# Row spreading on TensorE, shared PSUM banks, more weight gates, dummy matmuls and paired k r blocks in an RWKV5 plus squared-ReLU kernel

## The chip, the cores and the metric

The kernel runs on one core of one Trainium2 chip. The metric is the device time of one execution in microseconds (us). Each kernel is executed several times; I give the median and the range. A run counts as slow when it is more than 1.5% above the fastest run of the same kernel, and fast runs are compared with fast runs. The profile is one execution; its span is 1.8 us shorter than the device time of the same execution (before: 180.6 against 182.37 us).

Names of engines: PE is TensorE (matmul), PEld its weight loads, DVE VectorE, ACT ScalarE, POOL GpSimd, SP SyncE, which issues most loads. "Hardware queue" below is the queue of the loads that SP issues, "software queue" that of the weight slices, which POOL issues.

## The reference, cut to what matters

```python
# r, k, v: (4, 8, 768, 48) fp32;  w, u: (8, 48);  w_in: (384, 2048);  w_out: (2048, 384)
for t in range(S):
    kt, vt, rt = k[:, :, t], v[:, :, t], r[:, :, t]
    cur = einsum('bhd,bhe->bhde', u * kt, vt)
    y[:, :, t] = einsum('bhd,bhde->bhe', rt, state + cur)
    state = w * state + einsum('bhd,bhe->bhde', kt, vt)
x = y.transpose(0, 2, 1, 3).reshape(3072, 384)
h = maximum(x @ w_in, 0)
out = (h * h) @ w_out
```

The kernel cuts the sequence into 24 units: 6 chunks of 128 positions for each of 4 batches. Unit i is chunk i // 4 of batch i % 4. A unit needs k, r and v of its chunk. Its bonus term is `v * du`, where `du` is the sum over d of r k u. Two units make a pair, whose 256 rows go through the two feed-forward layers together.

## The kernel before

Nothing is scheduled by hand. The kernel describes each piece of work as a step with an engine, an estimated duration, the steps it needs, a priority, and the buffers that it takes (`alloc`) and gives back (`free`). A planner then plays a rough simulation and writes out the instructions in the order in which they started there.

```python
def order_steps(steps, pools, sw_rate=0.75, hw_rate=0.17):
    ...
        for e in ENGINES:
            ...
            for s in ready[e]:
                need = {}
                for _, p in s.alloc:
                    need[p] = need.get(p, 0) + 1
                if any(len(slots[p]) < n for p, n in need.items()):
                    continue                      # its buffers are not free yet
                if s.dma and out[e] >= 8:
                    continue
                if best is None or s.prio < best.prio:
                    best = s
    ...
    order.sort(key=lambda s: s.start)

PLAN = dict(per=6.2, loads=['k0', 'r0', 'v0', 'ub', 'k1', 'r1', 'v1', 'wcol',
            'kP1', 'rP1', 'vP1', 'kP2', 'rP2', 'vP2', ...],   # k0: of unit 0;  kP1: of units 2 and 3
            gates=[('v', 2), ('v', 2)], ..., lead=-1, f1lag=0.5, f2lag=8, ...)
POOLS = dict(ldr=2, ldk=2, ldv=2, rk=6, P0=4, ..., rkT=6, bank=3, bankH=3, bankO=2, Bm=3, ...)
```

A buffer of `ldv` holds v of a whole pair, one half for each unit. There are two of them, so pair 2 (units 4 and 5) takes the buffer of pair 0 (units 0 and 1). A load of a pair allocates its buffer:

```python
            Ld[x, 2 * p] = Ld[x, 2 * p + 1] = st(
                "ld" + item, "SP", 0.5, dma=2.05, alloc=[(var, "ld" + x)], emit=go, ...)
        else:
            def go(x=x, i=i, var=var):
                nc.sync.dma_start(out=ld[x][slot[var]][:, i % 2], in_=single[x][i % B, i // B])
            Ld[x, i] = st("ld" + item, "SP", 0.4, dma=1.04, prio=-150 + n, emit=go,
                          alloc=[(var, "ld" + x)] if i % 2 == 0 else [])
    ...
    for part in range(2):                        # the weights: two gates, four slices behind each
        ...
            nc.gpsimd.tensor_copy(gate[:, part : part + 1], ld[x][...][0:1, i % 2, 0, 0:1])
    ...
        dv[i] = st(f"dv{i}", "DVE", 0.56, [du[i], Ld["v", i], vb[i]], ...,     # v * du
                   free=[f"vP{g}"] if i % 2 else [], emit=f_dv(i))
        A = st(f"A{i}", "PE", 0.42, [rkT[i]], ...,                             # k r, 8 matmuls of 48 rows
               alloc=[(f"bA{i}0", "bank"), (f"bA{i}1", "bank")], emit=f_A(i))
```

A gate is a copy of one element of a load, written into POOL's order ahead of the weight slices, so that the slices are asked for only after that load has landed. In this kernel the only single loads are those of units 0 and 1.

Of the kernel before, what the change touches and what calls it, by code (L numbers as in the profile page):

```python
# [10 lines left out]
FP32 = mybir.dt.float32  # L11
# [4 lines left out]

class Step:
    def __init__(s, name, eng, dur, deps=(), prio=0.0, lat=0.08, alloc=(), free=(), dma=0.0, shared=False, emit=None):
        s.name = name
        s.eng = eng  # L20
        s.dur = dur
        s.deps = [d for d in deps if d is not None]
        s.prio = prio
        s.lat = lat
        s.alloc = list(alloc)
        s.free = list(free)
        s.dma = dma
        s.shared = shared
        s.emit = emit


ENGINES = ("PE", "ACT", "DVE", "POOL", "SP")


def order_steps(steps, pools, sw_rate=0.75, hw_rate=0.17):
# [14 lines left out]
    count = [0]  # L50

    def push(t, k, o):
        count[0] += 1
        heapq.heappush(ev, (t, count[0], k, o))
# [5 lines left out]
    slots = {k: list(range(n)) for k, n in pools.items()}  # L60
# [5 lines left out]
    clock = [0.0]  # L66
    order = []

    def rates():
        return (hw_rate, sw_rate) if rings["SP"] and rings["POOL"] else (1.0, 1.0)  # L70

    def advance(t):
        while clock[0] < t - 1e-9:
            if not rings["SP"] and not rings["POOL"]:
                clock[0] = t
                return
            rh, rs = rates()
            dt = t - clock[0]
            for q, r in (("SP", rh), ("POOL", rs)):
                if rings[q]:  # L80
                    dt = min(dt, rings[q][0][1] / r)
            clock[0] += dt
            for q, r in (("SP", rh), ("POOL", rs)):
                if rings[q]:
                    rings[q][0][1] -= dt * r
                    if rings[q][0][1] < 1e-7:
                        push(clock[0] + 1.2, "d", rings[q].pop(0)[0])

    def landing():
        rh, rs = rates()  # L90
        c = [rings[q][0][1] / r for q, r in (("SP", rh), ("POOL", rs)) if rings[q]]
        return clock[0] + min(c) if c else None
# [12 lines left out]
    while True:  # L105
# [5 lines left out]
        while ev and ev[0][0] <= t + 1e-9:  # L111
            _, _, k, o = heapq.heappop(ev)
            if k == "r":
                ready[o.eng].append(o)
            elif k == "f":
                slots[o[0]].append(o[1])
            elif k == "e":
                idle[o.eng] = True
                if not o.dma:
                    finish(o, t)  # L120
            elif k == "q":
                rings[o.eng].append([o, o.dma])
            elif k == "d":
                out[o.eng] -= 1
                finish(o, t)
        for e in ENGINES:
# [3 lines left out]
            for s in ready[e]:  # L130
                need = {}
                for _, p in s.alloc:
                    need[p] = need.get(p, 0) + 1
                if any(len(slots[p]) < n for p, n in need.items()):
                    continue
                if s.dma and out[e] >= 8:
                    continue
                if best is None or s.prio < best.prio:
                    best = s
# [15 lines left out]
            for v, p in s.alloc:  # L155
                where[v] = given[v] = (p, slots[p].pop(0))
            ready[e].remove(s)
            order.append(s)
            if s.dma:
                out[e] += 1  # L160
                push(s.end + 1.0, "q", s)
# [3 lines left out]
    return order, {v: i for v, (_, i) in given.items()}  # L165


PLAN = dict(per=6.2, loads=['k0', 'r0', 'v0', 'ub', 'k1', 'r1', 'v1', 'wcol', 'kP1', 'rP1', 'vP1', 'kP2', 'rP2', 'vP2', 'kP3', 'rP3', 'vP3', 'kP4', 'rP4', 'vP4', 'kP5', 'rP5', 'vP5', 'kP6', 'rP6', 'vP6', 'kP7', 'rP7', 'vP7', 'kP8', 'rP8', 'vP8', 'kP9', 'rP9', 'vP9', 'kP10', 'rP10', 'vP10', 'kP11', 'rP11', 'vP11'], nprep=8, p1set=2, nT=8, nX=8, gates=[('v', 2), ('v', 2)], sq=(1, 3, 5, 7), ldlead=26, lead=-1, f1lag=0.5, f2lag=8, relup=-3, sqp=-2)
POOLS = dict(ldr=2, ldk=2, ldv=2, rk=6, P0=4, dv=3, vb=8, rkT=6, bank=3, bankH=3, bankO=2, Bm=3, xs=3, xT=2, hr=6, hq=28, os=3, ts=2)
# [3 lines left out]
def kernel(  # L173
# [31 lines left out]
    def flat_rows(src):  # L205
        return bass.AP(tensor=src.tensor, offset=src.offset, ap=[[0, 128], [1, H * D]])
# [30 lines left out]
    first = {"bank": 0, "bankH": POOLS["bank"], "bankO": POOLS["bank"] + POOLS["bankH"]}  # L237

    def bank(var, pool):
        return banks[first[pool] + slot[var]]  # L240

    def heads(var, pool, n):
        return bank(var, pool).rearrange("p (a b) -> p a b", a=HP)[:, :, 0:n]
# [7 lines left out]
    wb = const.tile([128, H, D], FP32, name="wb")  # L251
    ub = const.tile([128, H, D], FP32, name="ub")
    wcol = const.tile([128, HP], FP32, name="wcol")
    logw = const.tile([128, H, D], FP32, name="logw")
    Wkhat = const.tile([128, H, D], FP32, name="Wkhat")
    Wt2 = const.tile([128, H, D], FP32, name="Wt2")
    WLm = const.tile([128, HP, 2 * D], FP32, name="WLm")
    gate = const.tile([1, 16], FP32, name="gate")

    tcol_i = const.tile([128, 1], mybir.dt.int32, name="tcol_i")  # L260
# [25 lines left out]
    nc.vector.memset(wcol, 1.0)  # L286
# [4 lines left out]
    steps = []  # L291
    PE_LAT = 0.25
    per = PLAN["per"]

    def st(name, eng, dur, deps=(), **kw):
        s = Step(name, eng, dur, deps, **kw)
        steps.append(s)
        return s

    def load_wcol():  # L300
        for e in range(2):
            nc.sync.dma_start(
                out=wcol[64 * e : 64 * e + D, :], in_=w.rearrange("(a e) d -> e d a", e=2)[e]
            )

    def make_WLm():
        nc.scalar.activation(wcol, wcol, AF.Ln)
        nc.scalar.activation(wcol, wcol, AF.Exp, scale=float(L))

    def fill_WLm():  # L310
        for e in range(2):
            col = wcol[64 * e : 64 * e + D, :]
            nc.gpsimd.tensor_copy(
                WLm[64 * e : 64 * e + D, :, D * e : D * (e + 1)],
                bass.AP(tensor=col.tensor, offset=col.offset, ap=[list(col.ap[0]), list(col.ap[1]), [0, D]]),
            )

    s_wb = st("wb", "SP", 0.1, dma=0.6, prio=-200, emit=lambda: nc.sync.dma_start(out=wb.rearrange("p a b -> p (a b)"), in_=flat_rows(w)))
    s_lw = st("logw", "ACT", 0.52, [s_wb], prio=-200, emit=lambda: nc.scalar.activation(logw, wb, AF.Ln))
    s_wk = st("Wk", "ACT", 0.61, [s_lw], prio=-199, emit=lambda: nc.scalar.activation(Wkhat, logw, AF.Exp, scale=njcol))  # L320
    s_wt = st("Wt", "ACT", 0.61, [s_wk], prio=-198, emit=lambda: nc.scalar.activation(Wt2, logw, AF.Exp, scale=tcol))

    Ld = {}
    where = {}
    n = 0
    for item in PLAN["loads"]:
        n += 1
        if item == "ub":
            Ld["ub"] = st("ub", "SP", 0.3, dma=0.6, prio=-150 + n, emit=lambda: nc.sync.dma_start(out=ub.rearrange("p a b -> p (a b)"), in_=flat_rows(u)))
        elif item == "wcol":  # L330
            Ld["wcol"] = st("wcol", "SP", 0.6, dma=0.3, prio=-150 + n, emit=load_wcol)
        elif item[1] == "P":
            x, p = item[0], int(item[2:])
            var = f"{x}P{p}"

            def go(x=x, p=p, var=var):
                nc.sync.dma_start(
                    out=ld[x][slot[var]].rearrange("p a h d -> p (a h) d"),
                    in_=both({"r": r, "k": k, "v": v}[x], p),
                )  # L340

            Ld[x, 2 * p] = Ld[x, 2 * p + 1] = st(
                "ld" + item, "SP", 0.5, dma=2.05, alloc=[(var, "ld" + x)], emit=go,
                prio=(2 * p - 2) * per - PLAN["ldlead"] + {"k": 0, "r": 0.1, "v": 0.2}[x],
            )
        else:
            x, i = item[0], int(item[1:])
            var = f"{x}P{i // 2}"

            def go(x=x, i=i, var=var):  # L350
                nc.sync.dma_start(out=ld[x][slot[var]][:, i % 2], in_=single[x][i % B, i // B])  # L351

            Ld[x, i] = st("ld" + item, "SP", 0.4, dma=1.04, prio=-150 + n, emit=go,
                          alloc=[(var, "ld" + x)] if i % 2 == 0 else [])

    s_wl = st("WLcol", "ACT", 0.45, [Ld["wcol"], s_wt], prio=-100, emit=make_WLm)
    s_wm = st("WLm", "POOL", 0.6, [s_wl], prio=-50, emit=fill_WLm)

    Ws = []
    for part in range(2):  # L360
        x, i = PLAN["gates"][part]

        def go(part=part, x=x, i=i):
            nc.gpsimd.tensor_copy(gate[:, part : part + 1], ld[x][slot[f"{x}P{i // 2}"]][0:1, i % 2, 0, 0:1])

# [351 lines left out]
```

## Time and profile before

| | before |
|---|---|
| median of 3 runs | 183.56 us (183.44 to 183.97) |
| span of the profiled run | 180.6 us |
| PE busy | 160.6 us, 89% of the span |
| granted clock, mean | 1.00 (no record before 28.22 us) |
| first matmul of the first layer | 27.48 us |
| weights' gate passed | 17.7 us |

These are lines of the profile's page: the busy time of each engine, the span in 40 equal slices (each digit is a busy share in tenths, PEclk the granted clock in tenths), and the chain of work that ended last.

```profile
span 180.6 us, 4082 instructions
PE 160.6 (89%) x1592; PEld 118.2 (65%) x1592; DVE 128.6 (71%) x216; ACT 117.5 (65%) x214; POOL 106.8 (59%) x116
...
PE   0344769899999999999999999999999999999991
...
DVE  3399998997388838959979696778777889631310
...
PEclk9999999999999999999999999999999999999999
...
PE 79%; DVE 9%; DMA 4%; ACT 2%; SPq 2%; issue 1%; DVEq 0%
```

From 40 us on (the tenth slice) PE is full, so work taken from PE there is time saved. Ahead of that VectorE is the full engine. The row PEclk says nothing of the start: the clock records in the trace of the kernel before begin only at 28.22 us, with full speed, and the views count the time ahead of the first record as full speed. The timeline shows otherwise: eight k r matmuls take 0.61 us at 23.21 us and 0.40 at 106.59. The table by stretches gives this more exactly; its columns are the stretch, its length, busy time of PE, PEld, DVE, ACT and POOL with the count of instructions, the granted clock, the DMA share (packet times summed over the time of 16 engines, so it can pass 1) and GB/s.

```profile
10.00:20.00 10.00, 5.33 (x53) 3.49 (x54) 9.87 (x17) 3.58 (x7) 6.54 (x10) 1.00 1.13 206
20.00:30.00 10.00, 7.92 (x86) 6.07 (x86) 9.08 (x17) 4.76 (x9) 9.84 (x11) 1.00 1.18 190
30.00:40.00 10.00, 8.93 (x97) 7.22 (x96) 9.49 (x19) 9.82 (x19) 2.13 (x3) 1.00 1.27 185
40.00:50.00 10.00, 10.00 (x94) 7.79 (x92) 5.98 (x10) 6.91 (x13) 6.77 (x7) 1.00 1.15 215
```

Three places of PE's timeline matter (start, duration, line, operation, tiles, shapes, count): the first first-layer matmuls, and a k r block between two others in the full stretch. The ends of matmuls are modelled, so block costs are read from start to start.

```profile
27.48 1.83 PE L604 MATMUL bank<-xT,W 128*128 128x256 bf16 x12
...
105.84 0.82 PE L604 MATMUL bank<-xT,W 128*128 128x256 bf16 x6
106.59 0.40 PE L454 MATMUL bank<-rkT 48*128 48x128 bf16 x8
106.92 0.82 PE L638 MATMUL bank<-W,hq 128*128 128x384 bf16 x4
```

The six matmuls at 105.84 are followed 0.75 us later by the k r block, whereas such a block followed by one of its own kind takes 0.655; the next block starts 0.33 later. A k r block of one unit costs 0.10 + 0.33 = 0.43 us.

### The profile page before, as it was taken

To read this page: it belongs to the slowest core of one execution; us is meant where nothing else is said; L and a number is where in the kernel's file an instruction comes from. 1 tells how busy PE (TensorE), PEld (TensorE's weight loads), DVE (VectorE), ACT (ScalarE), POOL (GpSimd) and SP (SyncE) were. 2 spreads that over 40 slices of the span, in tenths; PEclk is the share of its full clock that TensorE was granted. 3 is DMA by queue.
4 is the path that set the end of the run, shared out by engine and by line. 5 is a ranking of instruction groups with operands and counts; after the bars stand their busy time and mean duration, and the time that the engine had idled before them with its cause. 6 is when DMAs were issued, how large, how long until landed. Compare 5 with 4: busy or idle time off the path is not lost.

```text
span 180.6 us, 4082 instructions
## 1 busy us (share of the span) xinstructions
PE 160.6 (89%) x1592; PEld 118.2 (65%) x1592; DVE 128.6 (71%) x216; ACT 117.5 (65%) x214; POOL 106.8 (59%) x116
## 2 busy tenths in 40 slices
PE   0344769899999999999999999999999999999991
PEld 0222557778766867758678677677686776777760
DVE  3399998997388838959979696778777889631310
ACT  2641528986793886827776758579298495496851
POOL 2346998024940999599879977986968980000000
PEclk9999999999999999999999999999999999999999
DMA  3999999999949649979799799897896255221102
GB/s 85 207 195 216 196 191 193 184 185 222 225 116 241 149 82 253 184 152 241 142 216 204 122 237 202 138 225 164 167 228 155 71 120 80 65 65 47 41 2 87
DMA packets 105794, 28.44 MB, mean 157 GB/s; under 512 B 98864, under 2 KB 105776, under 8 KB 105776
## 3 DMA queue, kind: packets, MB, share of 16 engines
q1 hardware_dynamic: 102064, 25.04, 68.1%
q0 software_dynamic: 3712, 3.15, 11.0%
q8 instruction: 12, 0.20, 0.5%
q14 instruction: 6, 0.05, 0.1%
HBM read 20.84 MB, written 4.72 MB: 142 GB/s over the span
## 4 chain that ended last, share of the span: by engine, by line
PE 79%; DVE 9%; DMA 4%; ACT 2%; SPq 2%; issue 1%; DVEq 0%
PE bank L638 34%; PE bank L604 32%; PE bank L454 4%; PE bank L483 3%; DMA ub<-in_u_dram 2%; DMA xT<-xs 2%; PE bank L478 2%; PE bank L429 2%; DVE rk L382 2%; SPq L351 2%; DVE xs L506 2%; DVE dv L411 2%; PE bank L495 2%; DVE Bm L467 1%; ACT rkT L436 1%
## 5 line engine op out<-in xcount | busy, mean ns | idle before, releaser
L618 ACT ACTIVATE hr<-bank 128x512 bf16<-128x512 f32 x96 | 55.9, 595 | 29.4 <-PE bank L604 27.6
L604 PE MATMUL bank<-xT,W 128*128 128x256 bf16 x576 | 73.8, 273 | 0.4 <-DVE hq L629 0.3
L638 PE MATMUL bank<-W,hq 128*128 128x384 bf16 x384 | 72.0, 326 | 0.0
L604 PEld LDWEIGHTS <-W 128*128 128x128 bf16 x576 | 55.0, 98 | 11.8 <-issue 0.9
L638 PEld LDWEIGHTS <-hq 128*128 128x128 bf16 x384 | 36.1, 98 | 19.3
L629 DVE TENSOR_TENSOR hq<-bank,hr 128x512 bf16<-128x512 f32 x48 | 32.6, 683 | 17.4 <-ACT hr L618 17.4
L467 DVE TENSOR_TENSOR Bm<-bank,maskJT 128x512 bf16<-128x512 f32 x48 | 31.1, 681 | 8.2 <-PE bank L454 8.1
L388 POOL TENSOR_TENSOR P<-ldr,ldk 128x384 f32<-128x384 f32 x24 | 28.2, 1177 | 9.9 <-DMA ldr<-in_r_dram 9.9
L528 POOL TENSOR_TENSOR S0W<-ts,WLm 128x384 bf16<-128x384 f32 x16 | 16.5, 1031 | 29.1 <-DVE ts L522 28.9
L626 ACT ACTIVATE hq<-hr 128x512 bf16<-128x512 bf16 x48 | 30.2, 630 | 1.1
L397 POOL TENSOR_TENSOR P<-P,ub 128x384 f32<-128x384 f32 x22 | 22.9, 1043 | 1.4
L411 DVE TENSOR_TENSOR dv<-ldv,du 128x384 f32<-128x384 f32 x24 | 21.2, 883 | 0.5
L506 DVE TENSOR_TENSOR xs<-bank,dv 128x384 bf16<-128x384 f32 x24 | 13.3, 555 | 11.1 <-PE bank L483 10.7
L651 ACT COPY os<-bank 128x384 f32<-128x384 f32 x24 | 11.4, 476 | 12.4 <-PE bank L638 12.1
L429 PE MATMUL bank<-identity,rk 128*128 128x128 bf16 x64 | 7.5, 273 | 10.5 <-DVE rk L382 10.2
L382 POOL TENSOR_TENSOR rk<-ldr,Wt 128x384 bf16<-128x384 f32 x16 | 16.6, 1040 | 0.1
L382 POOL TENSOR_TENSOR rk<-ldk,Wkhat 128x384 bf16<-128x384 f32 x16 | 16.0, 1002 | 0.0
L429 PEld LDWEIGHTS <-rk 128*128 128x128 bf16 x64 | 5.5, 120 | 12.4 <-DVE rk L382 11.5
L417 ACT CAST vb<-ldv 128x384 bf16<-128x384 f32 x24 | 11.6, 507 | 2.9 <-DMA ldv<-in_v_dram 2.9
L403 DVE TENSOR_REDUCE du<-P 128x8 f32<-128x384 f32 x24 | 13.0, 543 | 0.2 <-POOL P L397 0.2
L454 PE MATMUL bank<-rkT 48*128 48x128 bf16 x192 | 10.6, 233 | 2.5 <-ACT rkT L436 2.2
L483 PE MATMUL bank<-vb,Bm 128*128 128x48 bf16 x192 | 12.2, 189 | 0.4 <-DVE Bm L467 0.4
(40 smaller groups left out, 101.7 us busy)
## 6 DMA issues: line engine op xcount, KB each, us to landing
out_dram<-os SPq DMA_DIRECT2D x24, 192.0 KB, 2.6
ldk<-in_k_dram SPq DMA_DIRECT2D x11, 384.0 KB, 4.1
ldr<-in_r_dram SPq DMA_DIRECT2D x11, 384.0 KB, 5.0
ldv<-in_v_dram SPq DMA_DIRECT2D x11, 384.0 KB, 4.0
W<-in_moe_w_in_dram POOLq DMA_DIRECT2D x4, 384.0 KB, 8.9
W<-in_moe_w_out_dram POOLq DMA_DIRECT2D x4, 384.0 KB, 15.6
ldk<-in_k_dram SPq DMA_DIRECT2D x2, 192.0 KB, 4.2
ldr<-in_r_dram SPq DMA_DIRECT2D x2, 192.0 KB, 4.5
```

Source lines behind the costliest of these rows:

```text
L382: e.tensor_mul(rk[slot[f"rk{i}"]][:, j, :, 0:D], ld[x][slot[f"{x}P{i // 2}"]][:, i % 2], tab)
L388: nc.gpsimd.tensor_mul(P0b[slot[f"P0{i}"]], ld["r"][slot[f"rP{i // 2}"]][:, i % 2], ld["k"][slot[f"kP{i // 2}"]][:, i % 2])
L397: (nc.vector if eng == "DVE" else nc.gpsimd).tensor_mul(t, t, ub)
L411: nc.vector.tensor_mul(dvb[slot[f"dv{i}"]], ld["v"][slot[f"vP{i // 2}"]][:, i % 2], du_b)
L454: nc.tensor.matmul(heads(f"bA{i}{e}", "bank", 128)[:, hc, :], rkT[p0 : p0 + D, HP + hc, :], rkT[p0 : p0 + D, hc, :], start=True, stop=True ...
L467: nc.vector.tensor_mul(Bmb[slot[f"Bm{i}"]][:, e], heads(f"bA{i}{e}", "bank", 128), mask_b)
L483: nc.tensor.matmul(Y[:, hc, D * e : D * (e + 1)], Bm[:, e, hc, :], vb[:, 2 * hc + e, :], start=(c == 0), stop=True, skip_group_check=True,)
L604: nc.tensor.matmul(hp[:, fi, :], W1[s // 2][:, c, 128 * f : 128 * (f + 1)], xt[:, c, :], start=(c == 0), stop=(c == CCH - 1), skip_group_c ...
L618: nc.scalar.activation(hrb[slot[f"hr{g},{s}"]], hp, AF.Relu)
L626: nc.scalar.activation(hq, hr, AF.Square)
L629: nc.vector.tensor_mul(hq, hp, hr)
L638: nc.tensor.matmul(o, hqb[slot[f"hq{g},{f // 2}"]][:, f % 2, L * j : L * (j + 1)], W2[q][:, f % 4, :], start=(f == 0), stop=(f == FCH - 1) ...
```

## The change

The intent is to begin the feed-forward part earlier and to make the k r blocks cheaper.

- w and u arrive as rows and are spread over the partitions by matmuls with a row of ones, instead of 128-row copies by DMA.
- All PSUM banks come from one list of eight, with shares (bank 4, bankH 4, bankO 3), instead of three fixed sets.
- Units 2 to 5 are loaded singly as well, in the order of need, and the eight weight slices have six gates instead of two: v of unit 2 for the first three slices, then one gate for each.
- Before the first layers begin, PE's gaps in the plan are filled with dummy matmuls on zeros.
- From unit 8 on, the k r products of two units are one block of 16 matmuls, in four banks.
- Lags and pools are tuned anew: `lead` -1 to -2, `f1lag` 0.5 to 0, `f2lag` 8 to 10; rk 6 to 4, rkT 6 to 4, Bm 3 to 2, P0 4 to 6, dv 3 to 6, xT 2 to 3.
- Two units fewer are transposed by PE (`nT` 8 to 6), and ScalarE makes 52 of the squares instead of 48.

The rest of the diff, about a thousand lines, turns closures into named functions. Its core:

```diff
@@ the planner's choice of a step @@
-                need = {}
-                for _, p in s.alloc:
-                    need[p] = need.get(p, 0) + 1
-                if any(len(slots[p]) < n for p, n in need.items()):
-                    continue
+                fits = True
+                if s.alloc:
+                    p = s.alloc[0][1]
+                    n = len(s.alloc)
+                    if p.startswith("bank"):
+                        fits = share[p] >= n and len(slots["banks"]) >= n
+                    else:
+                        fits = all(slots[p] for _, p in s.alloc)
...
-PLAN = dict(per=6.2, loads=['k0', 'r0', 'v0', 'ub', 'k1', 'r1', 'v1', 'wcol', 'kP1', 'rP1', 'vP1', 'kP2', 'rP2', 'vP2', ...
-            gates=[('v', 2), ('v', 2)], lead=-1, f1lag=0.5, f2lag=8, nT=8, ...)
+PLAN = dict(per=6.2, loads=['k0', 'r0', 'v0', 'k1', 'r1', 'v1', 'k2', 'r2', 'v2', 'k3', 'r3', 'v3', 'k4', 'r4', 'v4', 'k5', 'r5', 'v5', 'kP3', ...
+            gates=[('v', 2), ('v', 2), ('v', 2), ('k', 3), ('v', 3), ('k', 4), ('r', 4), ('v', 4)],
+            lead=-2, f1lag=0, f2lag=10, nT=6, nA=8, fill=24, ...)
...
+        if i < plan["nA"]:
+            A[i] = st(f"A{i}", "A", ((i,),), "PE", 0.43, ...)
+        elif i % 2 == 0:
+            A[i] = A[i + 1] = st(f"A{i}", "A", ((i, i + 1),), "PE", 0.66, [rkT[i], rkT[i + 1]], ...,
+                                 alloc=[(f"bA{j}{e}", "bank") for j in (i, i + 1) for e in (0, 1)])
...
+        if s.eng == "PE":
+            if s.start < min(opened, PLAN["fill"]):
+                cost = 0.45 if s.start < 5 else 0.24
+                for _ in range(int((s.start - before - 0.2) / cost)):
+                    nc.tensor.matmul(banks[7], warm[:, 0:128], warm, ...)
+            before = s.end
```

## The prediction

> **What bounds the kernel now.** From about 40 us on, TensorE (PE). The table by stretches has PE busy 10.0 of every 10 us from 40 to 160, save 9.65 in 80-90 and 9.9 in 150-160; the chain of waits gives PE 79% of the span. In the timeline a first-layer block (6 matmuls, 128x256) repeats every 0.655 us, a second-layer block (4, 128x384) every 0.65, a Y block 0.37, U 0.17; a k r block (8 matmuls on 48 rows) costs 0.43: it runs 0.33 after a 0.10 gap, though its weight loads take only 0.23. Times their counts (96, 96, 24, 20, 24, and 16 transpose blocks) that is about 153 us, my estimate of dense work. The other 27 us are start and tail. Before the first-layer matmuls begin at 27.4 us, PE does only 7 us of dense-rate work; VectorE is full there (9.9 of 10 us in 10-20, 9.1 in 20-30, 9.5 in 30-40). It waits 3.1 us for the decay table, then 1.65 for the 128-row copy of u. The weights' gate is passed at 17.7; their slices land 6.7 to 18.5 us after issue, the last near 42. The tail is 3.5 us after the last matmul.
>
> **What the change does.**
> 1. PE spreads w and u from rows: 0.39 MB leave the queue, about 2 us at 0.2 MB/us. The decay table comes no earlier, but unit 1's k and r do, and u stalls nothing.
> 2. Loads unit by unit, eight gates: the first slice is asked for at about 11.5, not 18.2; x of units 0 and 1 is done at about 18, not 21. In PE's order the first first-layer block stands behind unit 1 and the fourth rk transpose, not behind unit 3's U.
> 3. 26 dummy matmuls in gaps, all before that block. The Trainium skill's "TensorE: Matmul & The Clock Gate" (Part 1) says an idle array runs at half clock until about 3.4 us of sustained work. The trace agrees in effect: 8 k r matmuls take 0.61 us at 8.7 us, 0.40 later, though the granted clock reads 1.0. Worth below 1 us, as VectorE limits there.
> 4. Units 8 to 23: k r of two units in one block. The skill's "TensorEngine Tiling (Array Packing)", Key Properties, says a change of tiling mode drains the engine; the gap and the excess over 0.23 agree. A pair should cost 0.66, not 0.86: 1.6 us, wholly critical.
> 5. Two units fewer transposed on PE: 0.9 us. More early squares on ScalarE: 2.8 us of VectorE time.
>
> **Sum.** PE's dense work becomes 150.5 us, 4.4 of it before the first first-layer block, at about 19 us. Dense from there, PE would end at 165. Weights (2.5 to 2.8 us a slice beside loads, last near 35) and VectorE must hold it up in 19-36: I put 4.5 us, and 1 us for the four banks that a pair needs at once. PE ends at 170.5, span 174, plus 2.9 as before (183.56 against 180.6): **177 us**, range 172 to 181.5; faster by over 2%: 0.77, same 0.19, slower 0.04.
>
> **What would show it.** First first-layer matmul at 17-21 us; PE's end at 168-174, stretches from 40 us still full; blocks of 16 at about 0.66 us; weights landed near 35; the wait on u gone.
>
> **What would make it wrong.** Weights late because loads share the queue, so that PE is held on slices or on an x transpose queued ahead of ready blocks; pairs waiting for four banks; smaller pools (rk, rkT, masks) stalling PE after 40 us.

## More of the kernel before

The order in which instructions are written matters twice. Each engine executes its own instructions in that order. And an instruction that reads a buffer waits for the last write that stands ahead of it in that order.

## The result, and the profile after

The changed kernel takes 194.94 us (median of 4 fast runs, 194.13 to 195.66), and the kernel before, on the same chip, 183.74 us (183.44 to 183.97). The ratio is 1.061 with a 95% interval of 1.056 to 1.066: slower by 6%. A ratio in this document is the mean time of one kernel's fast runs over that of the other's of the same rounds, so it is not quite the ratio of the medians.

The same lines of the page, for the kernel after:

```profile
span 192.2 us, 4192 instructions
PE 166.8 (87%) x1620; PEld 121.1 (63%) x1622; DVE 120.7 (63%) x212; ACT 117.1 (61%) x218; POOL 104.8 (54%) x117
...
PE   7996000499999999999999999999999799999991
...
DVE  3943000879789669598897858969697774912210
...
PEclk9999755569999999999999999999999999999999
...
PE 79%; DMA 9%; DVE 4%; SPq 3%; POOL 2%; issue 1%; ACT 0%; DVEq 0%; POOLq 0%
```

VectorE stands still from 16.4 to 34.5 us and PE from 17.7 to 36.0, and the granted clock falls. After 40 us PE is nearly as full as before, except for one slice near 151 us. DMA has 9% of the chain of waits where it had 4%. Two lines of the table of waits (who waited for whom: total, times, longest) name the place; L543 is `v * du`, L571 the k r block, L581 the masking of its result.

```profile
PE bank L571 <- DVE Bm L581: 18.3, 1, 18.3
DVE dv L543 <- DMA ldv<-in_v_dram: 18.1, 1, 18.1
```

Each is one single wait. In VectorE's timeline (in brackets the idle time ahead of an instruction and what ended it):

```profile
15.89 0.54 DVE L538 TENSOR_REDUCE du<-P 128x8 f32<-128x384 f32 x1
34.50 0.82 DVE L543 TENSOR_TENSOR dv<-ldv,du 128x384 f32<-128x384 f32 x1 [18.07 <-DMA ldv<-in_v_dram]
```

VectorE takes its instructions in order, so the masks and x of every later unit wait behind it. The chain in order of time (start, duration, what) says which load it is; SPq L510 is the issuing of a load.

```profile
14.22 5.23 SPq L510
...
19.55 14.87 DMA ldv<-in_v_dram
...
34.50 0.82 DVE dv L543
```

And PE's timeline around the hole: the last dummies, the first k r block behind the hole, and the first first-layer block.

```profile
16.48 1.24 PE L698 MATMUL bank<-warm 128*128 128x512 bf16 x5
35.98 0.61 PE L571 MATMUL bank<-rkT 48*128 48x128 bf16 x8 [18.26 <-DVE Bm L581]
...
39.62 1.70 PE L647 MATMUL bank<-xT,W 128*128 128x256 bf16 x7
```

The first first-layer matmul starts at 39.6 us, 12.1 us later than before, and the run is 11.2 us longer. After it the two kernels go at nearly the same pace. The following table makes this visible. For each kernel I count the matmuls that PE has still to finish at a given time, multiply by what their blocks cost from start to start in a full stretch (first-layer block of six 0.655 us, second-layer block of four 0.65, Y 0.37 and 0.21 in the first chunk, U 0.17, k r 0.43 and 0.65 for a pair, the transposes of a unit 0.45 for r and k and 0.17 for x), and add the time itself. It is my estimate of where PE would end if it were dense from there. A number that rises is time lost in between.

| projected end of PE, us, seen at | 20 | 30 | 40 | 100 | 170 |
|---|---|---|---|---|---|
| before | 169.1 | 174.2 | 176.0 | 176.8 | 177.1 |
| after | 166.9 | 176.9 | 185.4 | 186.7 | 188.4 |

Seen at 20 us the kernel after is 2.2 us ahead, seen at 40 it is 9.4 behind, and at the end 11.3: nearly all of its loss falls between 20 and 40 us.

Which load does `v * du` of unit 1 (the instruction at 34.50) wait for? Unit 1's v was long there: ScalarE had cast it at 10.47 us. The load that landed at 34.4 was issued at 19.55, behind k and r of unit 5, and it is v of unit 5. The order in which the compiled kernel has them explains it. In the plan, unit 5's load of v stands at position 53, unit 1's product at 65, and unit 4's load of v, which allocates the pair's buffer, at 89. The load of unit 5 has no `alloc`, so the planner lets it go when SP is idle; its half of the pair's buffer is the half in which unit 1's v still lies. Since the load stands ahead of the product, the product waits for it. The trace has this edge itself: the product at 34.50 waits for semaphore 103, on which the loads of v of units 2 and 5 count, while unit 1's v counts on 110.

This is a wrong result, too. The product of unit 1 multiplies with unit 5's v. I worked out from the reference what that does: a relative L2 error of 0.071 on the unit's 128 rows and of 0.0147 on the whole output, which the comparison with the reference lets pass. No run showed this directly; it follows from the order of the instructions, and from the product's wait.

Theory: this one wrong edge, from the load of unit 5's v to the product of unit 1, holds VectorE, then PE, and lets PE's clock fall. It costs much only because that load lands late, among the weight slices. Rivals: (a) loads in general are late because the weights are now asked for at 11 us, so the hole would open elsewhere without the edge; (b) the dummies or the pairs hold the engines; (c) the smaller pools do.

### The profile page after: what moved, and what is told of

It is laid out like the page before. It is cut to its first block, busy times and chain, and to the rows that moved or that the text cites. A ratio compares the mean times of both kernels' runs of the same rounds, so it can differ in the third digit from the quotient of the medians.

```text
span 192.2 us, 4192 instructions
## 1 busy us (share of the span) xinstructions
PE 166.8 (87%) x1620; PEld 121.1 (63%) x1622; DVE 120.7 (63%) x212; ACT 117.1 (61%) x218; POOL 104.8 (54%) x117
## 4 chain that ended last, share of the span: by engine, by line
PE 79%; DMA 9%; DVE 4%; SPq 3%; POOL 2%; issue 1%; ACT 0%; DVEq 0%; POOLq 0%
PE bank L647 31%; PE bank L669 30%; DMA ldv<-in_v_dram 8%; PE bank L571 4%; PE bank L698 3%; SPq L510 3%; PE bank L593 2%; PE bank L589 2%; PE bank L555 2%; DMA rkT<-rk 2%; PE bank L602 2%; PE bank L462 1%; DVE dv L543 1%; DVE hq L664 1%; PE bank L628 1%
## 5 line engine op out<-in xcount | busy, mean ns | idle before, releaser
L669 PE MATMUL bank<-W,hq 128*128 128x384 bf16 x384 | 70.3, 326 | 0.1
L657 ACT ACTIVATE hr<-bank 128x512 bf16<-128x512 f32 x96 | 55.7, 596 | 19.6 <-PE bank L647 18.4
L664 DVE TENSOR_TENSOR hq<-bank,hr 128x512 bf16<-128x512 f32 x44 | 29.5, 683 | 18.7 <-ACT hr L657 18.4
L581 DVE TENSOR_TENSOR Bm<-bank,maskJT 128x512 bf16<-128x512 f32 x48 | 30.4, 683 | 13.5 <-PE bank L571 13.5
L623 POOL TENSOR_TENSOR S0W<-ts,WLm 128x384 bf16<-128x384 f32 x16 | 16.4, 1030 | 30.7 <-DVE ts L620 30.6
L662 ACT ACTIVATE hq<-hr 128x512 bf16<-128x512 bf16 x52 | 32.4, 630 | 1.0
L543 DVE TENSOR_TENSOR dv<-ldv,du 128x384 f32<-128x384 f32 x24 | 18.6, 778 | 18.7 <-DMA ldv<-in_v_dram 18.1
L535 POOL TENSOR_TENSOR P<-P,ub 128x384 f32<-128x384 f32 x23 | 25.0, 1088 | 9.0 <-DVE P L531 7.5
L571 PE MATMUL bank<-rkT 48*128 48x128 bf16 x192 | 9.1, 228 | 19.6 <-DVE Bm L581 18.3
L531 POOL TENSOR_TENSOR P<-ldr,ldk 128x384 f32<-128x384 f32 x22 | 23.2, 1055 | 5.2 <-DMA ldr<-in_r_dram 5.2
L679 ACT COPY os<-bank 128x384 f32<-128x384 f32 x24 | 11.3, 472 | 20.1 <-PE bank L669 19.9
L571 PEld LDWEIGHTS <-rkT 48*128 48x128 bf16 x192 | 5.9, 98 | 25.0 <-issue 22.1
L634 ACT COPY xT<-bank 128x384 bf16<-128x384 bf16 x8 | 3.7, 478 | 24.9 <-DVE Bm L581 21.3
L593 PE MATMUL bank<-vb,Bm 128*128 128x48 bf16 x192 | 11.2, 185 | 0.0
```

The lines of the kernel that those rows point to most:

```text
L531: engine(e).tensor_mul(P0b[slot[f"P0{i}"]], unit("r", i), unit("k", i))
L535: engine(e).tensor_mul(t, t, ub)
L543: nc.vector.tensor_mul(dvb[slot[f"dv{i}"]], unit("v", i), du_b)
L571: nc.tensor.matmul(heads(f"bA{i}{e}", 128)[:, hc, :], rkT[p0 : p0 + D, HP + hc, :], rkT[p0 : p0 + D, hc, :], start=True, stop=True, skip_g ...
L581: nc.vector.tensor_mul(Bmb[slot[f"Bm{i}"]][:, e], heads(f"bA{i}{e}", 128), mask_b)
L623: nc.gpsimd.tensor_mul(S0W[i % B], tsb[slot[f"ts{i}"]], WLm)
```

## The experiments

Thirteen kernels were run. The table shows them together; "before" is the kernel before in the same rounds.

| run | median us (range) | before us | ratio (95%) |
|---|---|---|---|
| e1_fix | 180.25 (179.12 to 181.41) | 183.03 | 0.985 (0.980 to 0.990) |
| e2_late | 182.04 (181.30 to 183.17) | 183.03 | 0.995 (0.991 to 1.000) |
| e3_fix_nodummy | 182.71 (181.66 to 182.86) | 183.03 | 0.997 (0.994 to 1.001) |
| e4_fix_nopair | 182.05 (181.06 to 183.87) | 183.03 | 0.993 (0.989 to 0.997) |
| e5_gates | 181.20 (180.46 to 181.96) | 183.15 | 0.990 (0.986 to 0.994) |
| e6_pools | 183.07 (180.10 to 183.28) | 183.15 | none: only one run counts as fast |
| e7_gates_pools | 181.91 (180.18 to 182.85) | 183.15 | 0.993 (0.987 to 0.999) |
| e8_gates_dummy | 181.91 (181.16 to 183.15) | 183.15 | 0.996 (0.990 to 1.001) |
| e9_prio | 178.21 (177.57 to 179.41) | 182.65 | 0.976 (0.969 to 0.982) |
| e10_loads | 181.87 (179.06 to 182.40) | 182.65 | 0.986 (0.977 to 0.996), two slow runs left out |
| e11_hybrid | 177.54 (177.42 to 178.33) | 182.65 | 0.972 (0.968 to 0.977) |
| e12_hybrid_nopair | 184.45 (183.62 to 185.37) | 183.06 | 1.005 (0.999 to 1.011) |
| e13_hybrid_nodummy | 179.97 (179.59 to 180.32) | 183.06 | 0.980 (0.974 to 0.985) |

In e4_fix_nopair, too, one of four runs (183.87) counts as slow and is left out of the ratio.

### e1_fix: the wrong edge taken away

```diff
-                fits = True
-                if s.alloc:
+                fits = s.kind != "load" or bool(s.alloc) or f"{s.args[0]}P{s.args[1] // 2}" in given
+                if fits and s.alloc:
```

The load of an odd unit is now held in the plan until the even unit's load has been given the pair's buffer. In the plan, VectorE's first 47 steps and the first 18 loads (w and u counted) are the same as before the edit.

> The planner may no longer choose an odd unit's load before its pair's buffer has been given out, so unit 5's load of v stands behind unit 1's product of v in the program instead of ahead of it; the first 48 instructions of VectorE and the first 18 loads are otherwise the same. Theory A (the 18.1 us wait of VectorE is one wrong edge: unit 1's product waits for unit 5's v): the wait at 16.4 us is gone, the granted clock stays 1.00, the first first-layer matmul comes at 18 to 22 us instead of 39.6, time 176 to 181 us. Theory B (the weights starve the loads, and any early gating does that): VectorE stops for 10 us or more at another load and the time stays above 187. The relative error also falls if theory A is right, because the changed kernel multiplies unit 1's weights with unit 5's v: worked out from the reference, that alone is a relative error of 0.0147 over the output.

The median is 180.25 us. The profiled run is its slowest, with a span of 179.5 us. VectorE's timeline at the same place, and PE's first first-layer block:

```profile
15.83 0.54 DVE L538 TENSOR_REDUCE du<-P 128x8 f32<-128x384 f32 x1
16.40 0.56 DVE L543 TENSOR_TENSOR dv<-ldv,du 128x384 f32<-128x384 f32 x1
...
21.30 1.47 PE L647 MATMUL bank<-xT,W 128*128 128x256 bf16 x12
```

The 18 us wait is gone, and the first layer begins at 21.3 us instead of 39.6. One edge in the order made the change 6% slower; without it the change is 1.5% faster than the kernel before (interval 1.0 to 2.0%). So the theory stands as to the loss, and rivals (b) and (c) don't explain it. Rival (a) is right about the remainder. Two lines show a smaller hole of the same kind, this time behind unit 5's r, which unit 5 does need: a wait in the table of waits, and the stretch in which it falls.

```profile
DVE rk L528 <- DMA ldr<-in_r_dram: 3.4, 2, 3.2
...
30.00:40.00 10.00, 7.24 (x53) 4.79 (x52) 4.74 (x9) 5.70 (x12) 3.16 (x4) 0.83 1.16 204
```

That load was issued at 13.79 us and landed at 33.89, after 20.1 us, beside the weight slices; the single loads of r have a median of 3.7 us in the kernel after. PE waits 2.8 us for it, and the granted clock of the stretch is 0.83.

The profiled run's late first layer is not the kernel's own. e4_fix_nopair and e9_prio, below, have the same first 87 steps in the same order, up to the first first-layer block, and there it starts at 18.64 and 19.19 us. In these three runs the difference goes with PE's clock: the first record of full speed is at 14.21 us in e1_fix, and at 8.54 and 9.05 in the other two. So single profiled runs of one and the same start differ by 2 to 3 us here, and smaller differences at the start are no finding.

### e2_late: the wrong edge kept, the weights asked for after it

```diff
-gates=[('v', 2), ('v', 2), ('v', 2), ('k', 3), ('v', 3), ('k', 4), ('r', 4), ('v', 4)]
+gates=[('v', 5)] * 8
```

Here the wrong edge stays (and the wrong product with it), but no weight slice is in flight while unit 5's v is loaded.

> The wrong edge is kept, but all eight weight gates wait for unit 5's v, so that its load has the queue to itself. Theory A with the weights as the amplifier: unit 1's product still waits for unit 5's v, but that lands at about 17 to 19 us, so the wait shrinks from 18.1 us to under 3; the weights are asked for at about 18 as in the kernel before; time 180 to 186. If the edge alone, without the weights, made the 18 us, the wait stays above 10 us and the time above 190.

The median is 182.04 us. The same instruction of VectorE now reads:

```profile
18.29 0.56 DVE L543 TENSOR_TENSOR dv<-ldv,du 128x384 f32<-128x384 f32 x1 [0.98 <-DMA ldv<-in_v_dram]
```

The wait for the same load is 0.98 us where it was 18.07. So the 18 us are the product of two things: the edge, and a load beside the weights. Either one taken away removes the loss. (Moving the gates also gives VectorE a new order from its 13th step on, so this run changes more than the time of the weights.) The granted clock of the profiled run is 1.00 from its first record, at 13.79 us, on. The price is that the weights are asked for at 18.4 us, about as late as in the kernel before (18.2), and the first layer begins at 25.1.

### e3_fix_nodummy: e1 without the dummies

```diff
-fill=24
+fill=0
```

> The mend of the first run, and no dummy matmuls. Theory A: VectorE sets the pace of the start, so the dummies are worth under 1 us: time within 1 us of the first run. A rival, that the half-rate clock matters: 2 us or more slower than the first run, with the early transposes and k r blocks at twice their length.

The median is 182.71 us, 2.5 us above e1_fix. The first transposes of r and k start at 6.20 us instead of 8.47, where in e1 eight dummies (3.59 us) hold them, and the first layer begins at 18.37 instead of 21.30 (18.64 in e4_fix_nopair). But twelve first-layer matmuls then take 2.76 us, against 1.47 in e1. So the dummies delay PE, and without them the half rate lasts into the first layer (the first clock record, at full speed, is at 21.80 us). But that is not shown to be the 2.5 us: in the projected end e3_fix_nodummy is 1.1 us ahead of e1_fix when seen at 40 us (170.9 against 172.0) and falls behind only after 100 us (177.2 against 175.9 at 170). What the dummies are worth at the start is better seen in e13_hybrid_nodummy.

### e4_fix_nopair: e1 with single k r blocks throughout

```diff
-nA=8
+nA=24
```

> The mend of the first run, and k r of each unit in a block of its own (24 blocks of 8). Theory: a pair saves one change of tiling mode, 0.2 us, on a full TensorE: 1.0 to 2.2 us slower than the first run. Rival (the pair's need of four free banks costs as much as it saves): within 0.5 us of the first run or faster.

The median of the three fast runs is 181.68 us (182.05 with the slow one): the pairs are worth 1.4 us on the medians, with ranges that overlap (179.1 to 181.4 and 181.1 to 182.4). The two kernels have the same order up to the 323rd step, yet their profiled starts differ as said above, so the medians alone prove little. The trace of e1_fix gives the size directly, in a full stretch of PE:

```profile
65.34 1.47 PE L647 MATMUL bank<-xT,W 128*128 128x256 bf16 x12
66.74 0.62 PE L571 MATMUL bank<-rkT 48*128 48x128 bf16 x16
67.30 0.94 PE L647 MATMUL bank<-xT,W 128*128 128x256 bf16 x7
```

Twelve first-layer matmuls cost 1.31 us, so they end at 66.65, and the next block starts at 67.30: the pair costs 0.65 us, where two single blocks cost 0.86. Eight pairs times 0.21 is 1.7 us. About half of the 0.21 is the gap of 0.09 ahead of the block, paid once instead of twice; the other half is that 16 matmuls run in 0.56 us and not in twice 0.33. The Trainium skill, "TensorEngine Tiling (Array Packing)", Key Properties, says that a change of tiling mode drains TensorE; the trace is in line with that and gives it a size, but shows the gap and not its reason.

### e5_gates: e1 with the second weight's slices behind unit 5's loads

```diff
-gates=[..., ('v', 3), ('k', 4), ('r', 4), ('v', 4)]
+gates=[..., ('r', 5), ('r', 5), ('v', 5), ('v', 5)]
```

If unit 5's r was late only because of the weights, holding back the second four slices should have shortened the hole.

> The mend of the first run, and the four slices of the second weight wait for unit 5's r and v instead of units 3 and 4. In the first run unit 5's r took 20 us to land behind the weights (issued 13.8, landed 33.9), VectorE waited 3.2 us for it and TensorE's clock fell to half. Theory (weights in front of the last early loads cost the rest of the start): that wait is gone, the granted clock stays 1.00, and the time is 1.5 to 4 us below the first run's 180.25. Rival (the queue is full either way, the order of its bytes only moves the wait to the second weight): within 1 us of the first run, with TensorE waiting before second-layer blocks.

The median is 181.20 us: no gain over e1_fix, and the step towards a faster kernel was a miss. VectorE's wait for r fell from 3.4 to 1.5 us, but PE now waits 2.3 us for a slice of the second weight, and PE is busy 7.8 of 10 us in 20 to 30 us as against 9.4, and 7.5 as against 7.2 in 30 to 40. From 20 to 40 us the queues carry 181 to 204 GB/s in both. What one load gains, a slice loses.

### e6_pools and e7_gates_pools: larger pools, alone and with the gates

```diff
-rk=4, ..., rkT=4, bank=4, Bm=2
+rk=6, ..., rkT=6, bank=4, Bm=3
```

> The mend of the first run with the buffers of before for rk, rkT and the masked products (6, 6 and 3 instead of 4, 4 and 2); the order of the instructions stays. Theory (the late gaps of TensorE at 77-80 and 111-116 us, about 3 us in the first run, come from transposes by DMA that start late because the smaller pools leave no lead): the gaps shrink and the time falls by 1 to 3 us. Rival (pools do not bind): within 0.7 us of the first run.

> Both of the two runs before this one. If the two effects are separate, their gains add: 176 to 178.5 us. If both only expose the same later wait, no better than the better of the two.

For e6_pools three of the four runs, the profiled one among them, count as slow, at 183.05 to 183.28 us, and one is 180.10. There is no ratio, and its trace is not used against fast ones. e7_gates_pools has 181.91 us, no better than e5_gates at 181.20. Larger pools by themselves bring nothing that these runs can show.

### e8_gates_dummy: e5 without the first dummies

```diff
-            if s.start < min(opened, PLAN["fill"]):
+            if 8.5 < s.start < min(opened, PLAN["fill"]):
```

This was meant to keep the later dummies and drop those that hold the first transposes.

> The gates of the fifth run, and the dummies planned before 8.5 us (10 of them) left out: in the first run eight of them hold the first transposes of TensorE from 6.3 to 8.5 us. Theory: unit 0's transposes start at 6.3 instead of 8.5, and the first first-layer matmul comes 1 to 2 us earlier; as VectorE and the loads set the rest of the start, time 0 to 1.5 us below the fifth run. Rival: without them the clock is still at half rate for the blocks up to about 18 us and the time is above the fifth run's by 1 us or more, as the run without any dummies was.

The median is 181.91 us against 181.20 for e5_gates: another miss. The first layer begins at 18.84 instead of 19.78, and nothing of it is left at the end.

### e9_prio: e1 with the lags of the kernel before

```diff
-lead=-2, f1lag=0, f2lag=10
+lead=-1, f1lag=0.5, f2lag=8
```

The change orders the attention of a unit and the two layers differently in time. In its full stretch e1_fix has PE waiting three times for a transpose by DMA to land: 0.40 us ahead of 79.95, 0.92 ahead of 111.73 and 1.00 ahead of 116.37.

> The mend of the first run with the three lags of before (lead -1, f1lag 0.5, f2lag 8), which decide how far the first-layer blocks stand behind the x that they read. Start and pairs stay. Theory (the late gaps of TensorE, 2.7 us in the first run, come from first-layer blocks that are queued with too little lead over their x transposes by DMA): the gaps after 70 us shrink below 1 us and the time is 178 to 179.5. Rival (the gaps come from the pairs or from the queue itself): gaps stay, time 179.5 to 182.

The median is 178.21 us, 2.0 us below e1_fix (other rounds, but the kernel before differs by only 0.4 us between them). The projected end tells where: e1_fix stands at 172.0 us when seen at 40 us and 175.9 at 170; e9_prio at 170.7 and 172.8. Of the 3.1 us between the two profiled runs, then, 1.3 are there by 40 us, where e1_fix had its late start, and 1.8 come later, where e9_prio has only one wait of 0.8 us for such a transpose left. (The profiled run of e1_fix is its slowest, so 3.1 is more than the 2.0 of the medians.)

### e10_loads and e11_hybrid: the start of the kernel before, and everything else of the change

e10_loads takes the edge away in another manner. The planner is left as the change has it, but units 2 to 5 are loaded in pairs again, so that each such load allocates its buffer; all weight slices are gated on v of unit 2.

```diff
-loads=[..., 'k2', 'r2', 'v2', 'k3', 'r3', 'v3', 'k4', 'r4', 'v4', 'k5', 'r5', 'v5', 'kP3', ...]
+loads=[..., 'kP1', 'rP1', 'vP1', 'kP2', 'rP2', 'vP2', 'kP3', ...]
-gates=[('v', 2), ('v', 2), ('v', 2), ('k', 3), ('v', 3), ('k', 4), ('r', 4), ('v', 4)]
+gates=[('v', 2)] * 8
```

> The changed kernel with its planner untouched, but with the loads of before (units 0 and 1 alone, then pairs) and one gate (unit 2's v) for all weights. Pairs have no odd unit whose load goes without a buffer, so this takes the wrong edge away in another way. Theory A: no long wait of VectorE on v, clock 1.00 for most of the start, first first-layer matmul at 19 to 24 us, time 179 to 183. If the time stays above 188, the single loads were not what held VectorE. Also: if the start is bound by the bytes of the weights and loads up to 40 us (theory from the gates run), single loads and eight gates are worth nothing and this run is within 1.5 us of the first run's 180.25.

Two of its four runs count as slow; the fast ones have 179.06 and 181.45 us. Its first layer begins at 20.96 us, 0.3 us earlier than in e1_fix. Both ways of removing the edge remove the loss.

e11_hybrid adds to e10_loads the lags of e9_prio and the pools of e6_pools, and `nT=8`, the eight units transposed on PE as in the kernel before. What remains of the change are the rows spread by PE, the shared banks, the weights asked for some 3.5 us earlier (14.76 us against 18.23), the dummies, more squares on ScalarE, the larger pools P0, dv and xT, and the pairs.

> The run before this one with the lags, the buffers and the eight transposed units of before as well, so that what is left of the change is mainly the spread of w and u, the dummies, the shared banks and the pairs. Theory: pairs are worth 1.6 us and the start about 1 us, the late gaps go: 179 to 181. Rival: pairs need four banks and leave the gaps whatever the lags: 181.5 to 184.

The median is 177.54 us, the fastest of all, below the 179 to 181 expected, and 2.8% faster than the kernel before. The span is 175.7 us, the clock 0.999.

### e12_hybrid_nopair and e13_hybrid_nodummy: what the pairs and the dummies are worth there

```diff
-nA=8                 # e12_hybrid_nopair
+nA=24
-fill=24              # e13_hybrid_nodummy
+fill=0
```

> The hybrid (177.54 us, 177.42 to 178.33, its runs close together) with k r of each unit in a block of its own, 24 blocks of 8. If a pair saves one change of tiling mode of 0.2 us on a full TensorE, 8 pairs are worth 1.6 us: 178.8 to 179.6. If the pairs' need of four banks gives it back: within 0.6 us of the hybrid.

> The hybrid without dummy matmuls. The prediction put them below 1 us; the mended kernel without them was 2.5 us slower, but its trace showed the loss in late gaps and not in the start. If the half-rate clock is what it costs, the hybrid is slower by 1.5 to 3 us with TensorE's blocks at twice their length up to about 20 us. If the start is bound by loads and weights whatever TensorE does, within 1 us of the hybrid.

e12_hybrid_nopair has 184.45 us, 6.9 us above e11_hybrid. That is not the worth of the pairs, since most of it is lost before any pair. ScalarE stood, in order, on a load of v. The first line is of e12_hybrid_nopair, the second the same instruction in e11_hybrid:

```profile
32.69 0.51 ACT L546 CAST vb<-ldv 128x384 bf16<-128x384 f32 x1 [4.84 <-DMA ldv<-in_v_dram]
30.22 0.51 ACT L546 CAST vb<-ldv 128x384 bf16<-128x384 f32 x1 [1.21 <-DMA ldv<-in_v_dram]
```

PE waited 3.65 us for an x that ScalarE had still to copy, and the clock fell to 0.50 in 35 to 40 us. In the projected end, e12_hybrid_nopair is 6.1 us behind e11_hybrid already at 40 us (177.0 against 170.9); 1.7 of that are the pairs still to come, which the count knows, and 4.4 are lost by then, though e11_hybrid issues its first pair only at 62.93 us. The order of the start is not the reason: run again, the planner gives both kernels the same first 281 steps in the same order and buffers, up to 55 us of the plan. What differs is when things happened. In e12_hybrid_nopair the first eight transposes took 1.00 us instead of 0.61, this load of v was issued 0.44 us later and the first weight slice 0.48 us earlier, and the load landed 2.5 us later, at 32.67 us. Why the two starts differ is not shown; the four times of each kernel lie close together, so it isn't one odd execution. The run is confounded as a measure of the pairs, and it is instructive all the same: it is the loss of the kernel after in a smaller edition, without any wrong edge.

e13_hybrid_nodummy has 179.97 us, so the dummies are worth 2.4 us, with the same order of all steps. In both kernels PE must wait for the first weight slice. First the lines of e13_hybrid_nodummy, then those of e11_hybrid:

```profile
22.71 1.46 PE L647 MATMUL bank<-xT,W 128*128 128x256 bf16 x6 [3.91 <-DMA W<-in_moe_w_in_dram]
24.11 0.61 PE L571 MATMUL bank<-rkT 48*128 48x128 bf16 x8
```

```profile
21.17 0.83 PE L647 MATMUL bank<-xT,W 128*128 128x256 bf16 x6 [1.76 <-DMA W<-in_moe_w_in_dram]
21.93 0.40 PE L571 MATMUL bank<-rkT 48*128 48x128 bf16 x8
```

Without dummies the same six matmuls take 1.46 us instead of 0.83, and the k r block 0.61 instead of 0.40, until about 28 us. Seen at 40 us the projected ends are 172.9 and 170.9: 2.0 us are lost by then. Half rate need not be all of it: the first slice also landed 1.55 us later (22.67 against 21.12), beside a load of v that was issued at 14.74 instead of 15.31 us and landed at 23.54 instead of 30.20. The two parts were not separated. The granted-clock view reads 1.00 for both kernels, because the records begin at 28.10 us here and at 8.05 in e11_hybrid.

## Why the prediction was right or wrong, point by point

Predicted were 177.0 us (172 to 181.5), and measured 194.94. The prediction was wrong.

**The step that failed** is the second, and with it the sum: the first first-layer matmul "at about 19" us, and "4.5 us" for weights and VectorE holding PE up in 19 to 36. Measured: 39.6 us, and VectorE held for 18.1 us by one wait. The prediction treated the order of loads as a list of needs, each engine waiting only for what it uses. The compiled order of the kernel after has unit 1's product wait for unit 5's load. With the edge gone the first layer starts about as predicted (18.64 and 19.19 us in e4_fix_nopair and e9_prio, 21.30 in the slow start of e1_fix), so it was this wait that the step lacked. That could have been read before the run from the plan: run by itself, the planner puts unit 5's load of v at position 53, ahead of unit 1's product at 65, into the same half of a buffer. The prediction looked at PE's order ("the first first-layer block stands behind unit 1 and the fourth rk transpose") and not at VectorE's waits.

**A named risk that was half of the cause.** "Weights late because loads share the queue" was the first of the reasons for being wrong. It was the other way round: a load on the hardware queue was late because of weight slices on the software queue. The Trainium skill, "DMA: Bandwidth & Descriptors", Issuing engines are not separate DMA queues, says that DMAs from different engines run on the same 16 DMA engines and interleave. The trace agrees: unit 5's v took 14.9 us from issue to landing in the kernel after, unit 5's r 20.1 us in e1_fix, against a median of 3.6 to 3.7 us for single loads of k and r. e2_late shows the converse, a wait of 0.98 us.

**The clock.** The Trainium skill, "TensorE: Matmul & The Clock Gate", Part 1, says that an array idle for a window of about 3.4 us goes to half clock, and that sustained work brings it back. Once PE stood still, that took its part, which the prediction had not foreseen since it foresaw no standstill. These rows of the table by stretches are of the kernel after:

```profile
20.00:22.00 2.00, 0.00 (x0) 0.00 (x0) 0.00 (x0) 0.00 (x0) 1.37 (x2) 0.79 1.19 185
22.00:36.00 14.00, 0.02 (x2) 0.02 (x3) 1.50 (x3) 0.00 (x0) 6.85 (x8) 0.50 1.09 168
36.00:40.00 4.00, 3.78 (x35) 2.89 (x36) 4.00 (x9) 0.61 (x2) 1.05 (x3) 0.50 0.59 67
40.00:42.00 2.00, 2.00 (x15) 1.44 (x13) 1.07 (x3) 1.48 (x2) 0.00 (x0) 0.59 1.28 238
42.00:50.00 8.00, 8.00 (x105) 6.67 (x104) 7.27 (x15) 7.61 (x15) 0.00 (x0) 1.00 0.64 124
```

PE's last dummies start at 16.48 us and end at 17.72. The clock is half from 21.18 us, after 3.5 us without work, and it is full again from 41.66, 5.7 us after work resumed at 35.98.

**What was right.** PE's dense work bounds the kernel from 40 us on: in the kernel after, too, the projected end moves by only 3.0 us in the 130 us from 40 to 170 (before: 1.1). A pair was to cost 0.66 us and costs 0.65; 1.6 us in all were predicted, and e4_fix_nopair against e1_fix shows 1.4 on the fast runs, in ranges that overlap. The wait on u is gone. The weights are asked for at 11.1 us, as predicted ("about 11.5").

**What was mis-sized.** The dummies were to be worth "below 1 us, as VectorE limits there", and are worth 2.4 us (e13_hybrid_nodummy against e11_hybrid): the half rate reached into the first layer, and the first slice came later as well. The 2.5 us between e3_fix_nodummy and e1_fix were not lost at the start and don't bear on this. And the losses after the start were put too low. The prediction had PE dense from 19 us, ending at 165, plus 4.5 us up to 36 and 1 us for the banks: 170.5. In the profiled run of e1_fix PE ends at 175.9, and the 5.4 us between are, by my estimate, 1.1 by 20 us (the late start of that run; e9_prio stands at 164.9 there), 1.4 between 20 and 40 (5.9 instead of 4.5) and 2.9 after that (3.9 instead of 1). On the medians 3.25 us remain (180.25 against 177.0), since the profiled run is the slowest, and since the prediction added 2.9 us from span to time where this run has 1.9. The rise between 20 and 40 us is common to all. This is the projected end for mended kernels, made as above:

| projected end of PE, us, seen at | 20 | 30 | 40 | 100 | 170 |
|---|---|---|---|---|---|
| before | 169.1 | 174.2 | 176.0 | 176.8 | 177.1 |
| e1_fix | 166.1 | 167.3 | 172.0 | 173.4 | 175.9 |
| e5_gates | 165.4 | 168.0 | 172.4 | 174.0 | 175.5 |
| e9_prio | 164.9 | 166.3 | 170.7 | 171.1 | 172.8 |
| e11_hybrid | 166.3 | 169.6 | 170.9 | 171.5 | 172.1 |
| e13_hybrid_nodummy | 166.3 | 172.0 | 172.9 | 172.9 | 174.7 |

In every one of the five mended kernels the end moves out by 4.6 to 7.0 us between 20 and 40 us (before: 6.9), whichever way loads and slices are ordered, while DMA moves 181 to 204 GB/s at a share above 1 in all five. PE is busy 16.60 us of those 20 in e1_fix, which waits for r, and 16.55 us in e11_hybrid, which waits for weight slices. So I take the start to be bound by the bytes of weights and loads together. That is argued from these rows and from the miss of e5_gates, and not shown; no run took bytes away, and it stays open how much less data would gain.

**What stays open.** The wrong product was shown by order and wait, and not by a comparison of outputs. The worth of the shared banks and of the rows spread by PE was not measured by itself, nor that of `nT=8`. Nor does any run here show why PE's clock is first full at 7.86 to 9.77 us in some profiled runs with the same first dummies and at 13.79 to 14.35 in others (e1_fix, e2_late, the kernel after). e11_hybrid's 177.54 us agree with the predicted 177 by accident: it is another kernel, and its terms are not those of the sum.

## What to carry to other kernels

When a planner writes out the order of instructions, look before anything else at what each instruction waits for in the compiled order, on the in-order engines above all: a load that goes into part of a shared buffer must be tied to the giving back of that buffer, or it gets an edge nobody meant, and perhaps wrong data that a tolerant comparison lets pass. Asking for weights early is not free for loads that are already in flight or come behind them, so find the instruction that will stand on the slowest of those loads, and ask what stands behind it. And when one knob of such a plan is changed, compare the stretch ahead of the knob's first effect in both traces: where the orders are still the same, a difference of several us there is not the knob's.

## What the Trainium skill lacked or had wrong

- "TensorE: Matmul & The Clock Gate", Part 1, describes the half clock after idleness, and the runs agree with it. It also warns that the clock's events in a profile can be unreliable; but neither it nor another page I read says that they can be missing at the start. Here the records begin at 28.22 us (before), 28.10 (e13_hybrid_nodummy) and 8.05 (e11_hybrid), and a view that counts the time ahead of them as full speed reads 1.00, while six first-layer matmuls take 1.46 us at 22.7 us in e13_hybrid_nodummy and 0.83 in e11_hybrid.
- The same section says that for modeling the ramp costs under 1% of a typical span. Here the dummies that keep PE awake are worth 2.4 of 177.5 us, 1.4%, in spite of the transposes that they delay; some of this may be the first weight slice, which landed 1.55 us later without them.
- "TensorEngine Tiling (Array Packing)", Key Properties, says that a change of mode drains the engine, and gives no figure. Here one k r block costs 0.43 us and a pair 0.65, so what is saved by one block fewer is about 0.2 us.
- "DMA: Bandwidth & Descriptors" says that queues interleave, and in its section on queues and rings that an engine takes turns between them, a packet at a time; it gives no figure for what this does to one load. Here a 192 KB load on the hardware queue took 14.9 and 20.1 us beside 384 KB slices on the software queue, against a median near 3.7 us.
